# Sliding-window attention and a gated convolution layer on one core: tanh kept in PSUM, diagonals built later, and new parameters for the written-out order

## The chip, the cores and the metric

The kernel runs on one core of one Trainium2 chip. A core has a matrix engine (TensorE, PE in the profile), a vector engine (VectorE, DVE), a scalar engine (ScalarE, ACT), a general engine (GpSimd, POOL), and an engine that here only issues transfers (SyncE, SP). The metric is the device time of one launch in microseconds; the time given is the median of several runs. TensorE writes its results into PSUM, here one tensor `pf` of 4096 float32 columns that the kernel treats as eight banks of 512; everything else lies in SBUF.

## What is computed

Eight batches of windowed attention (eight heads, 576 positions, head size 64, each position sees the 32 on each side), and behind it a two-layer network whose hidden layer is gated by a three-tap convolution over positions:

```python
scores = np.where(np.abs(pos[:, None] - pos[None, :]) <= 32, q @ k.T / 8, -1e9)
x = softmax(scores) @ v                  # (8, 576, 512), heads side by side
h = np.maximum(x @ w_in, 0.0)            # 512 -> 1024
conv = sum(conv_w[t] * shifted(h, t - 1) for t in range(3))   # along the positions, zero at the ends
out = (h / (1.0 + np.exp(-conv))) @ w_out                     # 1024 -> 512
```

Inputs and output are float32; the matrix products are done in bfloat16. The sigmoid is taken as tanh: with `h` halved when it is evicted, `h * sigmoid(conv)` is `(tanh(conv / 2) + 1) * h / 2`.

## The kernel before, in words

**Units.** The 8 x 576 rows are cut into twelve chunks of 384 (`CH`), three to a pair of batches. The hidden layer is made transposed, d_ff on partitions, in eight blocks of 128 (`m`). One block of one chunk is a unit (`unit`, line 740); chunk 1 is worked in two halves of 192, because its first half needs batch 0 alone and its second batch 1. A unit is this chain:

- `ph`: 4 TensorE matmuls from `xT` and `w_in_sb` into a PSUM bank (`ps`), line 761
- `relu`: ScalarE evicts that bank into `hT`, halved, line 772
- `pc`: the convolution as matmuls with diagonal matrices (`diag_w`) into a second bank (`pc`), line 793. In chunks 0 and 1 all three taps; in the others (`TAP`, line 297) taps 0 and 2 only
- `tap`: for the others VectorE adds the middle tap into the bank, one scalar_tensor_tensor that reads and writes PSUM, line 804
- `tanh`: ScalarE reads the bank and writes `tn`, one of five float32 buffers in SBUF, line 813; the bank is free when it ends
- `gate`: VectorE makes `gT = (tn + 1) * hT`, line 818

When a chunk's eight units are there, `project` (line 829) multiplies `gT` by `w_out_sb` in three blocks of 128 rows, 8 matmuls of 512 columns each, ScalarE or VectorE evicts `y`, and SP stores it.

**Attention.** For each batch (`attention`, line 888) and each half of the heads: q and k are loaded into a ring of four buffers `st`, cast to bfloat16 (`cast_qk`, into `qkb`), transposed by TensorE (`transposes`, two banks for each of q and k) and evicted into `qkT`. `scores` takes three banks in a row for each of two parts, ScalarE writes exp into `attn`, VectorE multiplies by the mask. v is loaded into one buffer `vst`, cast into `ve` (`cast_v`), and copied once more, shifted by 64 partitions, into `vo` (`shift_v`, on VectorE). `values` multiplies, VectorE takes the reciprocal of the sums (`rec`) and scales into `xn`. `turn` makes `xT`: for batches 0 to 2 with TensorE and an eviction, for the others with a transposing DMA.

**What sets the order.** Nothing is scheduled while the kernel runs: each engine executes one fixed list. The lists come from `Planner` (lines 93 to 277), which runs when the kernel is built. Each piece of work is an `op` with a priority number (smaller is more urgent), a cost on each engine that may do it, the data that it reads and writes, the buffers that it takes and those that it uses. The planner plays the work through with modelled times: whenever an engine is free it takes the most urgent op that is ready and whose buffers, PSUM banks among them, are free at that moment. So the priority numbers, the costs and the buffer counts decide which instruction stands behind which. A bank is taken when the op that writes it is placed, and given back when the last op that uses it is done. Further rules of it:

- An op marked `two` isn't placed on VectorE while the plan has a `two` op on GpSimd, nor the other way round (`lock`). Casts, the masks, the shifted copies, the diagonals and, when `tn` is in SBUF, the gate are marked (line 825).
- On TensorE an op whose mode (`row`, `col`, none) differs from the last op's has `SWITCH` added to its priority.
- Where TensorE has nothing to do in the first 23 us (`FILL`), it is given dummy matmuls on zeros.
- A unit of chunk `c` has priority `8 c + m`, its later ops up to 0.7 more; the projection of chunk `c` has `8 (c + 1)` plus `PYAT`. A batch's attention lies between the two numbers of `place` (line 883), its steps at fixed tenths of that stretch; its loads come 12 before it.
- All loads and stores, and the transposing DMAs, are issued by SP in the planned order. SP waits for each one's buffer before it goes to the next.

The diagonals are made by `diag` ops (line 874), three multiplications of the identity each, for `m` from 0 to 7, right after the convolution weights have come, with priorities -20 to 5.

Of the kernel before, what the change touches and what calls it, by code (L numbers as in the profile page):

```python
# [92 lines left out]
class Planner:  # L93
# [4 lines left out]
    SWITCH = 0.1  # L98
# [30 lines left out]

    def run(self, start, filler, filler_until, late):  # L130
# [43 lines left out]
        for o in self.ops:  # L174
            if not o.left:
                push(0.0, "ready", o)
# [4 lines left out]
        while left or heap:  # L181
# [7 lines left out]
            for kind, x in batch:  # L189
                if kind == "ready":  # L190
                    offer(x)
                elif kind == "free":
                    x.give(now, 7, 1)
                elif kind == "done":
                    for s in x.uses:
                        s.users -= 1
                        if not s.users:
                            s.pool.give(now, s.index, s.span)
                    for n in x.after:
                        n.left -= 1  # L200
                        if not n.left:
                            push(now, "ready", n)
# [3 lines left out]
            for e in engines:  # L206
                while free[e] <= now + 1e-9:
                    best, blocked = None, False
                    other = {"DVE": "POOL", "POOL": "DVE"}.get(e, "PE")
                    for o in todo[e]:  # L210
                        if o in gone:
                            continue
                        if o.two and lock[other] > now + 1e-9:
                            blocked = True
                            continue
                        need = {}
                        for s in o.acquire:
# [3 lines left out]
                        key = o.prio + (self.SWITCH if e == "PE" and o.mode != mode else 0.0)  # L221
# [23 lines left out]
                    for n in o.follow:  # L245
                        n.left -= 1
                        if not n.left:
                            push(now, "ready", n)
# [32 lines left out]
START = {"SP": 0.9, "PE": 2.5, "ACT": 1.2, "DVE": 4.5, "POOL": 4.5}  # L281
FILL = 23.0
THIN = 2.0
NHT = 6
NTN, NQKT, NY = 5, 3, 3
NRING, NATTN, NGT, NQKB = 4, 3, 2, 6
LOADV1, LOADWO, CASTWO = -89.0, -89.5, 6.0
TN_SBUF = True
MASKER = ("DVE",)
ENGW = ("POOL", "ACT")  # L290
ENG1 = ("POOL", "DVE")
TAP0 = 1
AHEAD = 0
XD0 = 3
PYAT = (2.0, 4.5, 7.0)


def TAP(c, m):
    return c > TAP0


def XDMA(b):
    return b >= XD0


SH2, SHX = -2.0, -6.0
# [3 lines left out]
def kernel(  # L310
# [48 lines left out]
    ring = pool("st", NRING, [128, 2, 2, RP, 64], FP32)  # L359
    vst = sb.tile([128, NBLK, H, 64], FP32, name="vst")  # L360
    qkb = pool("qkb", NQKB, [128, RP, 2, 64], BF16)
    qkT = pool("qkT", NQKT, [128, 4, W], BF16)
    ve_b = [sb.tile([128, NBLK, H, 65], BF16, name=f"ve{i}") for i in range(2)]
    vo_b = [sb.tile([128, NBLK - 1, H, 65], BF16, name=f"vo{i}") for i in range(2)]
    attn_p = pool("attn", NATTN, [128, 36 * 64], BF16)
    rec_p = pool("rec", 4, [128, 4], FP32)
    xn_p = pool("xn", 2, [128, NBLK, H, 64], BF16)
    xT_b = [sb.tile([128, KC, 2, S], BF16, name=f"xT{i}") for i in range(2)]
    hT_p = [pool(f"hT{i}", NHT, [128, CH + (4 if i == 1 else 2)], BF16) for i in range(3)]
    gT_p = pool("gT", NGT, [128, MB, CH], BF16)  # L370
    tn_p = pool("tn", NTN, [128, CH], FP32) if TN_SBUF else None
    y_p = pool("y", NY, [128, d_model], FP32)
# [61 lines left out]
    pl.psum = pf  # L434
    op = pl.op

    def masker(b):
        costs = {"DVE": c_dve(1152, 2.0), "POOL": c_pool(1152, 2.6)}
        return {e: costs[e] for e in (("DVE",) if b < 2 else MASKER)}
# [65 lines left out]
    def cast_v(b, c, prio, engines):  # L505
        def emit(e):
            copier(e, ve_b[b % 2][:, c, :, 0:64], vst[:, c, :, :])
        op(f"cast v{b}{c}", cast_cost(512, engines), emit, prio,
           reads=[("vst", c)], writes=[("ve", b % 2, c)], two=True)

    def shift_v(b, c0, c1, prio):
# [3 lines left out]
        def emit_hi(e):  # L515
            vector.tensor_copy(out=vo[0:64, c0:c1], in_=ve[64:128, c0:c1])

        def emit_lo(e):
            vector.tensor_copy(out=vo[64:128, c0:c1], in_=ve[0:64, c0 + 1:c1 + 1])
        for emit, w, r in ((emit_hi, "hi", 0), (emit_lo, "lo", 1)):  # L520
            op(f"vo {w}{b}{c0}", {"DVE": c_dve(n, 4.0)}, emit, prio, two=True,
               reads=[("ve", b % 2, c + r) for c in range(c0, c1)],
# [42 lines left out]
    def transposes(b, i, y, prio, ahead):  # L565
# [4 lines left out]
        parts = 2 if ("qkb", b, i, y, 1) in pl.writer else 1  # L570
        turned = lambda x: ps[x].ap.bitcast(BF16)[:, 0:S]
        for n, js in enumerate(((0, 1, 2, 3), (4, 5, 6, 7, 8))):
            def emit(e, js=js):
                for j in js:
# [6 lines left out]
            o = op(f"tr {'qk'[y]}{b}{i}.{n}", {"PE": 0.03 * len(js)}, emit, prio, mode="row",  # L581
                   reads=[("qkb", b, i, y, min(n, parts - 1)), "ident"], writes=[("ptr", b, i, y, n)],
# [9 lines left out]
        for x in range(2):  # L592
            op(f"ev {'qk'[y]}{b}{i}.{x}", evac_cost(S), lambda e, x=x: emit_ev(e, x),
               prio + 0.05, reads=[("ptr", b, i, y, n) for n in range(2)], writes=[("qkT", b, i, y, x)],
# [49 lines left out]
    def values(b, i, c, prio, ahead, engines):  # L644
# [10 lines left out]
        def emit(e_):  # L655
# [12 lines left out]
            reads=[("attn", b, x, z) for x in halves for z in range(2)] + [("ve", b % 2, c)]  # L668
# [25 lines left out]
    def turn(b, c, prio, ahead):  # L694
# [5 lines left out]
        if XDMA(b):  # L700
# [39 lines left out]
    def unit(c, m, part, prio):  # L740
# [40 lines left out]
        op(f"relu {u}", {"ACT": c_act(n)}, emit_relu, prio + 0.1, reads=[("ph", u)], writes=[("h", u)], use=[ps, hT])  # L781
# [8 lines left out]
        on_dve = TAP(c, m)  # L790
# [20 lines left out]
        tn = Slot(tn_p) if TN_SBUF else pc  # L811

        def emit_tanh(e_):
            scalar.activation(tn.ap[:, 0:nc_], pc.ap[:, 0:nc_], AF.Tanh, bias=0.0, scale=1.0)
        op(f"tanh {u}", {"ACT": c_act(nc_)}, emit_tanh, prio + 0.6, reads=[("tap" if on_dve else "pc", u)],
           writes=[("tanh", u)], use=[pc], acquire=[tn] if TN_SBUF else [])

        def emit_gate(e_):
# [6 lines left out]
           use=[tn, hT, gT], two=TN_SBUF)  # L825
# [37 lines left out]
    def conv_weights(prio):  # L863
# [9 lines left out]
        for m in range(MB):  # L873
            def emit_d(e_, m=m):
# [6 lines left out]
               reads=["conv_w"], writes=[("diag", m)], two=True)  # L881

    place = {0: (-30.0, -10.0), 1: (1.0, 9.0), 2: (11.0 + SH2, 21.0 + SH2), 3: (21.0 + SHX, 31.0 + SHX),
             4: (34.0 + SHX, 46.0 + SHX), 5: (46.0 + SHX, 54.5 + SHX), 6: (57.0 + SHX, 69.0 + SHX),
             7: (69.0 + SHX, 78.5 + SHX)}
    loads = {b: -100.0 + 10.0 * b if b < 2 else place[b][0] - 12.0 for b in place}

    def attention(b):
        w0, w1 = place[b]
        early = b < 2  # L890
        ahead = 0 if b == 0 else AHEAD
        any3 = ("POOL", "DVE", "ACT")
        step = (w1 - w0) / 10.0
        lp = loads[b]
# [3 lines left out]
        for c in range(NBLK):  # L898
            load_v(b, c, (loads[b] if b != 1 else LOADV1) + 0.05 + 0.01 * c)
        for i in range(2):  # L900
            for y in range(2):
                cast_qk(b, i, y, w0 + step * (3 * i - 3.0), any3 if b == 0 else ENG1 if b == 1 else ("POOL",),
                        ((0, 4), (4, 9)) if b == 0 else ((0, 9),))
        for c in range(NBLK):
            cast_v(b, c, w0 + step * (2.0 + 0.2 * c), any3 if b == 0 else ENG1 if b == 1 else ("POOL",))
        if early:
            for c in range(NBLK - 1):
                shift_v(b, c, c + 1, w0 + step * (2.5 + 0.2 * c))
        else:
            shift_v(b, 0, NBLK - 1, w0 + step * 3.5)  # L910
        for i in range(2):
            for y in range(2):
                transposes(b, i, y, w0 + step * (2.8 * i + 0.9 * y), ahead)
            scores(b, i, w0 + step * (2.8 * i + 2.3), ahead)
        if early:
            for c in range(NBLK):
                for i in (range(2) if c < NBLK - 1 else (None,)):
                    values(b, i, c, w0 + step * (6.8 + 0.6 * c), ahead, ("DVE", "ACT"))
                turn(b, c, w0 + step * (7.4 + 0.6 * c), ahead)
        else:  # L920
            for i in range(2):
                for c in range(NBLK - 1):
                    values(b, i, c, w0 + step * (5.0 + 2.3 * i), ahead, ("DVE",))
            values(b, None, NBLK - 1, w0 + step * 7.3, ahead, ("DVE",))
            for c in range(NBLK):
                turn(b, c, w0 + step * 9.5, ahead)

    conv_weights(-60.0)
    for pr_ in range(B // 2):
        attention(2 * pr_)  # L930
        if pr_ == 0:
            for i in range(2):
                load_w("in", i, -99.0 + i * 0.1)
            for m in range(MB):
                cast_w("in", m, -9.0 + m, ("POOL", "DVE", "ACT"))
        attention(2 * pr_ + 1)
        if pr_ == 0:
            for i in range(2):
                load_w("out", i, LOADWO + i * 0.1)
            for m in range(MB):  # L940
                cast_w("out", m, CASTWO + 0.1 * m, ENGW)
        for c in range(3 * pr_, 3 * pr_ + 3):
# [3 lines left out]
            for i in range(3):  # L946
                project(c, i, 8.0 * (c + 1) + PYAT[i] if c < NCH - 1 else 8.0 * c + 3.6 + 0.1 * i)

    order = pl.run(START, (0.107, "filler", THIN), FILL, pf)
# [37 lines left out]
```

## Time and profile before

| | |
|---|---|
| runs | 246.98, 247.8, 248.75 us; median 247.8 |
| the profiled execution | 248.0 us; span from first to last instruction 246.2 us; granted TensorE clock 0.991 |
| busy | PE 224.6 us, weight loads 130.7, DVE 205.8, ACT 179.6, POOL 76.8 |
| moved | 32.52 MB read, 9.44 MB written, 65984 packets on the queue of SP |
| first unit's first matmul | at 25.8 us |
| last eviction of y | starts at 241.8 us |

In the profile L349 is the line of a helper through which every engine's operation passes, so groups are told apart by what they write and read: `gT<-tn,hT` is a gate. `[1.57 <-DVE qkT L349]` behind a row is idle time of the engine before it and what ended it. A row with `x12` is that many instructions, merged; its time runs from the first start to the last end. In tables of stages the columns are start and end, length, then busy microseconds of each engine with its number of instructions, the granted TensorE clock as a share, the mean busy share of the DMA engines (modelled, so it can pass 1), and GB/s.

### The profile page before, as it was taken

Reading aid. Unit: us, or ns where it says so; the run is one execution under the profiler, and the core shown is the slowest. Engines: PE = TensorE matmul, PEld = TensorE weight load, DVE = VectorE, ACT = ScalarE, POOL = GpSimd, SP = SyncE. Lnnn points to the kernel's source line nnn. Section 1 sums busy time; section 2 is a strip of 40 time slices with the busy share of each in tenths; the row PEclk is TensorE's granted clock in tenths of the full one; section 3 lists DMA queues with packets and bytes.
Section 4 is the critical chain, followed back from the end, with each engine's and each line's share of the span. In section 5 each row is a group of like instructions: output and inputs, shape, how many; then the busy total and the mean of one; then the engine's idle time right before and its main releaser. Section 6 shows DMA issues by size and latency. Waiting matters only on the chain.

```text
span 246.2 us, 7187 instructions
## 1 busy us (share of the span) xinstructions
PE 224.6 (91%) x2765; PEld 130.7 (53%) x2789; DVE 205.8 (84%) x457; ACT 179.6 (73%) x432; POOL 76.8 (31%) x108
## 2 busy tenths in 40 slices
PE   7787999699999599989999999999999999999981
PEld 4465557476655355455555555555555555555430
DVE  6989379999899979979998999899988985849342
ACT  3496999598997436889849858986698676757431
POOL 4326646866747313513650231350000000000000
PEclk9999999999999889999999999999999999999999
DMA  6999999999999169749973893961522233020213
GB/s 212 287 284 391 236 295 246 337 230 353 254 330 270 36 192 337 144 119 312 296 159 67 187 324 76 233 188 44 110 82 83 62 77 129 14 88 30 85 45 128
DMA packets 66054, 45.37 MB, mean 184 GB/s; under 512 B 51148, under 2 KB 51172, under 8 KB 66020
## 3 DMA queue, kind: packets, MB, share of 16 engines
q1 hardware_dynamic: 65984, 44.90, 65.5%
q8 instruction: 22, 0.36, 0.6%
q14 instruction: 12, 0.10, 0.1%
q10 hardware_dynamic: 36, 0.01, 0.1%
HBM read 32.52 MB, written 9.44 MB: 170 GB/s over the span
## 4 chain that ended last, share of the span: by engine, by line
PE 50%; DVE 6%; ACT 5%; issue 3%; ACTq 0%; DVEq 0%
PE pf L349 50%; ACT tn L349 2%; DVE pf L349 2%; ACT attn L349 2%; DVE xn L349 2%; DVE gT L349 1%; DVE rec L349 1%; ACT hT L349 1%; ACT qkT L349 1%; DVE attn L349 1%; ACTq L982 0%; ACT y L349 0%; DVEq L349 0%; ACTq L349 0%; DVE vo L349 0%
## 5 line engine op out<-in xcount | busy, mean ns | idle before, releaser
L349 PE MATMUL pf<-xT,w_in_sb 128*128 128x385 bf16 (+2 forms) x416 | 76.2, 317 | 0.8 <-DVE xn L349 0.6
L349 DVE SCALAR_TENSOR_TENSOR gT<-tn,hT 128x384 bf16<-128x384 f32 (+1 forms) x104 | 63.0, 627 | 12.2 <-ACT tn L349 11.4
L349 PE MATMUL pf<-w_out_sb,gT 128*128 128x512 bf16 x264 | 65.8, 381 | 2.6 <-DVE gT L349 0.9
L349 ACT ACTIVATE tn<-pf 128x384 f32<-128x384 f32 (+1 forms) x104 | 50.0, 515 | 18.8 <-DVE pf L349 17.9
L349 ACT ACTIVATE hT<-pf 128x385 bf16<-128x385 f32 (+2 forms) x104 | 50.6, 530 | 11.8 <-PE pf L349 10.9
L349 DVE SCALAR_TENSOR_TENSOR pf<-hT,conv_w_sb,pf 128x384 f32<-128x384 bf16 x80 | 47.7, 617 | 12.9 <-PE pf L349 11.9
L349 POOL TENSOR_SCALAR qkb<-st 128x1152 bf16<-128x1152 f32 (+2 forms) x32 | 38.7, 1211 | 50.6 <-DMA st<-in_k_dram 18.7
L349 PEld LDWEIGHTS <-w_in_sb 128*128 128x128 bf16 x416 | 38.6, 98 | 24.5 <-issue 2.5
L349 PE MATMUL pf<-hT,diag_w 128*128 128x384 bf16 (+1 forms) x232 | 48.1, 312 | 1.6 <-ACT hT L349 1.0
L349 PEld LDWEIGHTS <-gT 128*128 128x128 bf16 x288 | 27.6, 98 | 31.8 <-DVE gT L349 1.7
L349 ACT ACTIVATE attn<-pf 128x512 bf16<-128x512 f32 (+1 forms) x96 | 41.9, 555 | 2.9 <-PE pf L349 2.7
L349 POOL TENSOR_SCALAR ve<-vst 128x512 bf16<-128x512 f32 x38 | 28.1, 751 | 28.5 <-DMA vst<-in_v_dram 27.4
L349 ACT COPY y<-pf 128x512 f32<-128x512 f32 x32 | 18.9, 594 | 19.1 <-PE pf L349 18.6
L349 DVE TENSOR_TENSOR attn<-attn,mask 128x1152 bf16<-128x1152 bf16 x32 | 29.2, 916 | 2.1 <-ACT attn L349 1.6
L349 PEld LDWEIGHTS <-diag_w 128*128 128x128 bf16 x232 | 20.1, 98 | 15.1 <-issue 2.7
L349 ACT COPY qkT<-pf 128x576 bf16<-128x576 bf16 x41 | 27.2, 715 | 0.8 <-PE pf L349 0.7
L349 DVE TENSOR_TENSOR xn<-pf,rec 128x256 bf16<-128x256 f32 x64 | 23.3, 409 | 0.1
L349 PE MATMUL pf<-ve,attn 128*64 128x65 bf16 x320 | 15.7, 198 | 4.9 <-ACT attn L349 3.1
L349 PEld LDWEIGHTS <-attn 128*64 128x64 bf16 x576 | 12.3, 112 | 13.9 <-issue 6.0
L349 DVE COPY qkT<-pf 128x576 bf16<-128x576 bf16 x23 | 17.1, 751 | 2.9 <-PE pf L349 1.5
L349 DVE COPY vo<-ve 64x520 bf16<-64x520 bf16 (+1 forms) x28 | 17.7, 631 | 0.9
L349 PEld LDWEIGHTS <-qkT 64*128 64x128 bf16 x576 | 10.9, 95 | 10.5 <-issue 7.0
(39 smaller groups left out, 138.6 us busy)
## 6 DMA issues: line engine op xcount, KB each, us to landing
st<-in_q_dram SPq DMA_DIRECT2D x16, 576.0 KB, 6.2
st<-in_k_dram SPq DMA_DIRECT2D x16, 576.0 KB, 6.8
out_dram<-y SPq DMA_DIRECT2D x36, 256.0 KB, 2.7
vst<-in_v_dram SPq DMA_DIRECT2D x24, 256.0 KB, 8.5
vst<-in_v_dram SPq DMA_DIRECT2D x16, 192.0 KB, 5.8
st<-in_moe_w_in_dram SPq DMA_DIRECT2D x2, 1024.0 KB, 7.9
st<-in_moe_w_out_dram SPq DMA_DIRECT2D x2, 1024.0 KB, 9.1
xT<-xn SPq DMA_TRANSPOSE x30, 2.5
```

The lines of the kernel that those rows point to most:

```text
L349: return lambda *args, **kwargs: fixed(do(*args, **kwargs))
```

## The change

Buffers and plan, before and after:

| | before | after |
|---|---|---|
| `tn` buffers | 5 in SBUF | none: tanh is written back into the unit's own PSUM bank, and the gate reads it there; the gate is no longer marked `two` |
| `qkb`, `attn`, `xn`, `y` buffers | 6, 3, 2, 3 | 5, 4, 3, 4 |
| `hT`, `st`, `qkT`, `gT`, `rec` buffers | 6, 4, 3, 2, 4 | the same |
| diagonals for `m` of 2 to 7 | as soon as the weights are there | not before 22.25 in the plan's time |
| middle tap on VectorE | chunks 2 to 11, all eight blocks | the same, but for one block of chunk 8 |
| `SWITCH` | 0.1 | 0.05 |
| VectorE's start in the plan | 4.5 | 5.0 |
| planned cost of `relu` | for n columns | for n + 20 |
| batches 2 to 7 in the plan | 9-19, 15-25, 28-40, 40-48.5, 51-63, 63-72.5 | 10.0-20.0, 16.0-26.0, 30.3-41.2, 36.3-46.3, 51.7-63.7, 66.8-70.7 |
| batch 1 | 1-9 | -0.55-8.91 |
| loads ahead of a batch | 12 | 11.49 |
| casts of q and k, batch 1 / later | POOL or DVE / POOL | POOL / POOL or ACT |
| casts of v, batch 1 / later | POOL or DVE / POOL | POOL, DVE or ACT / POOL |
| casts of `w_in` / `w_out` | POOL, DVE or ACT / POOL or ACT | POOL or ACT / POOL, DVE or ACT |
| transposes of a half's q or k, after batch 0 | two ops (blocks 0-3, 4-8) | one op |
| `PYAT` | 2.0, 4.5, 7.0; last chunk 3.6 | 2.31, 4.75, 7.61; last chunk 2.16 |

The steps inside a batch (casts, transposes, scores, values, turning) also have new offsets for batch 0, batch 1 and the others. The core of the diff:

```diff
     def op(self, name, cost, emit, prio, reads=(), writes=(), reserve=(), acquire=(), use=(),
-           spare=0, mode=None, two=False, behind=None):
+           spare=0, mode=None, two=False, behind=None, early=0.0):
         o = Op(name, cost, emit, prio, list(acquire), spare, mode, two)
+        o.early = early
...
-                            push(now, "ready", n)
+                            push(max(now, n.early), "ready", n)
...
+P = {'start': {'SP': 0.9, 'PE': 2.5, 'ACT': 1.2, 'DVE': 5.0, 'POOL': 4.5},
...
+ 'diag': 22.25,
...
+ 'switch': 0.05,
+ 'hT': 6,
+ 'st': 4,
+ 'qkb': 5,
+ 'qkT': 3,
+ 'attn': 4,
+ 'gT': 2,
+ 'tn': 0,
+ 'y': 4,
+ 'xn': 3,
+ 'rec': 4,
...
+ 'at': ((-30.0, -10.0), (-0.55, 8.91), (10.03, 20.04), (15.96, 26.04), (30.29, 41.16), (36.31, 46.33), (51.71, 63.72),
+        (66.77, 70.71)),
...
+ 'lead': 11.49,
+ 'v1': -89.27,
+ 'w_in': (-99.0, -98.9),
+ 'w_out': -89.74,
+ 'cast_w_in': -0.86,
+ 'cast_w_out': -1.65,
+ 'e_qk': (('POOL', 'DVE', 'ACT'), ('POOL',), ('POOL', 'ACT')),
+ 'e_v': (('POOL', 'DVE', 'ACT'), ('POOL', 'DVE', 'ACT'), ('POOL',)),
+ 'e_vo': (('DVE',), ('DVE',), ('DVE',)),
+ 'e_mul': (('DVE', 'ACT'), ('DVE', 'ACT'), ('DVE',)),
...
+ 'tap': (0, 0, 8, 8, 8, 8, 8, 8, 7, 8, 8, 8),
+ 'xdma': 3,
+ 'py': (2.31, 4.75, 7.61),
+ 'py_last': 2.16}
...
-        tn = Slot(tn_p) if TN_SBUF else pc
+        tn = Slot(tn_p) if P["tn"] else pc
...
         op(f"tanh {u}", {"ACT": c_act(nc_)}, emit_tanh, prio + 0.6, reads=[("tap" if on_dve else "pc", u)],
-           writes=[("tanh", u)], use=[pc], acquire=[tn] if TN_SBUF else [])
+           writes=[("tanh", u)], use=[pc], acquire=[tn] if P["tn"] else [])
...
         op(f"gate {u}", {"DVE": c_dve(nc_)}, emit_gate, prio + 0.7, reads=[("tanh", u)], writes=[("g", c, m, part)],
-           use=[tn, hT, gT], two=TN_SBUF)
+           use=[tn, hT, gT], two=P["tn"])
...
             op(f"diag {m}", {"DVE": (0.31, 0.39)}, emit_d, -20.0 + m if m < 3 else m - 2.0,
-               reads=["conv_w"], writes=[("diag", m)], two=True)
+               reads=["conv_w"], writes=[("diag", m)], two=True, early=0.0 if m < 2 else P["diag"])
```

More of the change, by code (lines that the diff above doesn't have):

```diff
@@ L505, in cast_v, with emit @@
     def cast_v(b, c, prio, engines):
[L506 to L509, printed above, removed]
+        n = H // P["vparts"]
+        for z in range(P["vparts"]):
+            def emit(e, z=z):
+                copier(e, ve_b[b % 2][:, c, n * z:n * z + n, 0:64], vst[:, c, n * z:n * z + n, :])
+            op(f"cast v{b}{c}.{z}", cast_cost(512 // P["vparts"], engines), emit, prio,
+               reads=[("vst", c)], writes=[("ve", b % 2, c, z)], two=True)
     def shift_v(b, c0, c1, prio):
@@ L593, in transposes @@
             op(f"ev {'qk'[y]}{b}{i}.{x}", evac_cost(S), lambda e, x=x: emit_ev(e, x),
-               prio + 0.05, reads=[("ptr", b, i, y, n) for n in range(2)], writes=[("qkT", b, i, y, x)],
+               prio + 0.05, reads=[("ptr", b, i, y, n) for n in range(len(parts))], writes=[("qkT", b, i, y, x)],
                use=[ps[x], to])
@@ L890, in attention @@
         early = b < 2
-        ahead = 0 if b == 0 else AHEAD
-        any3 = ("POOL", "DVE", "ACT")
+        kind = min(b, 2)
+        ahead = P["ahead"][kind]
         step = (w1 - w0) / 10.0
-        lp = loads[b]
+        o = P["off"][kind]
+        at = lambda k, n=0.0: w0 + step * (o[k] + n)
+        lp = -100.0 + 10.0 * b if early else w0 - P["lead"]
         for i in range(2):
```

154 lines of the change are left out of this document (82 added, 72 removed).

## The prediction

> **What bounds the kernel now.** I read the page first, then the busy time by stage.
>
> ```profile
> span 246.2 us, 7187 instructions
> PE   7787999699999599989999999999999999999981
> ```
> ```profile
> 0.00:26.00 26.00, 20.45 (x307) 13.61 (x308) 21.76 (x78) 16.52 (x43) 11.81 (x41) 1.00 1.00 299
> 26.00:50.00 24.00, 21.68 (x328) 13.97 (x329) 18.97 (x34) 21.17 (x58) 16.07 (x18) 1.00 1.00 270
> 50.00:80.00 30.00, 28.68 (x499) 19.00 (x499) 28.57 (x58) 27.79 (x81) 19.55 (x21) 1.00 1.08 289
> 80.00:90.00 10.00, 7.19 (x75) 3.89 (x75) 8.29 (x18) 3.82 (x10) 2.41 (x5) 0.83 0.38 108
> 90.00:150.00 60.00, 57.55 (x738) 32.27 (x745) 56.61 (x124) 46.01 (x102) 21.47 (x21) 1.00 0.78 209
> 150.00:200.00 50.00, 49.14 (x619) 27.60 (x625) 46.20 (x104) 39.75 (x91) 5.52 (x7) 1.00 0.42 109
> 200.00:236.00 36.00, 35.85 (x191) 18.77 (x194) 21.39 (x39) 21.77 (x48) 0.00 (x0) 1.00 0.19 65
> ```
>
> Columns: stage, length, then busy us of PE, weight load, DVE, ACT, POOL, then granted clock, DMA share, GB/s. PE looks full from 50 us on, but its matmuls overlap, so I count its work by the distance between starts in the dense last stage:
>
> ```profile
> 204.88 1.89 PE L349 MATMUL pf<-w_out_sb,gT 128*128 128x512 bf16 x8
> 206.61 0.81 PE L349 MATMUL pf<-hT,diag_w 128*128 128x384 bf16 x4
> 207.26 2.14 PE L349 MATMUL pf<-xT,w_in_sb 128*128 128x385 bf16 x12
> ```
> ```profile
> 32.73 0.44 PE L349 MATMUL pf<-ident,qkb 64*128 64x64 bf16 x18
> ```
>
> Less the last one's own length (0.38, 0.33, 0.33, 0.19), a matmul costs 0.216, 0.16, 0.165 and 0.015 us. A unit (one of eight 128-row blocks of d_ff in a chunk) is 4 first-layer matmuls, 2 taps and 3 of the output projection: 0.66 + 0.32 + 0.65 = 1.63 us. There are 96 units (the 16 half units count as 8): 156 us. Chunks 0 and 1 have a third tap: 16 x 0.16 = 2.6. Attention per batch is 72 transposes, 72 scores and 72 value products; at 0.015 each 3.2 us, seven batches after the first 23. Together 182 us, in the 215 us between 26 and 241. So PE has about 33 us of hidden slack, and DVE, whose durations are real, is busy 94% from 50 to 80 and from 90 to 150, and 92% from 150 to 200, but 59% from 200 to 236. DVE's order of work is the bound from 50 to 200; PE alone is from 200 on; until 50 the loads are (DMA share 1.00).
>
> **Part 1: the gate reads tanh from PSUM.** Forms, then smallest/median/largest ns:
>
> ```profile
> L349 DVE SCALAR_TENSOR_TENSOR gT<-tn,hT 128x384 bf16<-128x384 f32 x88 | 53.9, 630 | 11.8 <-ACT tn L349 11.0
> L349 DVE SCALAR_TENSOR_TENSOR gT<-tn,hT 128x192 bf16<-128x192 f32 x16 | 9.2, 610 | 0.4 <-ACT tn L349 0.4
> ```
> ```profile
> L349 ACT ACTIVATE tn<-pf x104: 365/490/808, 28.5 to 239.7; 128x384 f32<-128x384 f32 x88, 128x192 f32<-128x192 f32 x16
> L349 DVE SCALAR_TENSOR_TENSOR gT<-tn,hT x104: 344/558/1498, 29.0 to 240.2; 128x384 bf16<-128x384 f32 x88, 128x192 bf16<-128x192 f32 x16
> L349 DVE SCALAR_TENSOR_TENSOR pf<-hT,conv_w_sb,pf x80: 600/617/625, 68.5 to 239.0; 128x384 f32<-128x384 bf16 x80
> L349 DVE TENSOR_TENSOR xn<-pf,rec x64: 387/414/424, 17.9 to 195.4; 128x256 bf16<-128x256 f32 x64
> L349 DVE COPY qkT<-pf x23: 743/751/761, 7.9 to 184.1; 128x576 bf16<-128x576 bf16 x23
> ```
>
> The gate has two SBUF inputs and spreads from 344 to 1498 ns; the tap, the scaling into xn and the DVE copy, each with one operand in PSUM, stay within 40 ns of each other, in the same stages, beside the same POOL casts. The long gates end where POOL ends:
>
> ```profile
> 24.00:50.00 26.00, 7.81 (x10) 5.75 (x13) 1.00 1.01 280
> 50.00:100.00 50.00, 14.28 (x23) 9.33 (x22) 0.97 0.91 248
> 100.00:150.00 50.00, 14.59 (x23) 11.51 (x24) 1.00 0.74 198
> 150.00:200.00 50.00, 13.59 (x25) 12.18 (x24) 1.00 0.42 109
> 200.00:240.00 40.00, 12.18 (x22) 11.09 (x23) 1.00 0.19 65
> ```
>
> These are the gates (DVE) and tanh (ACT) alone. After 200, where POOL does nothing, a gate takes 12.18/22 = 0.554 us. Up to 150 there are 56 gates in 36.68 us; 16 of them are halves. Undisturbed they would be 40 x 0.554 + 16 x 0.344 = 27.7 us, so 9.0 us are lost to POOL: 2.7 of them before 50 (8 x 0.554 + 2 x 0.344 = 5.1 of 7.81) and 6.3 from 50 to 150.
>
> With tanh in PSUM the gate has one SBUF input. Its price is not in the trace. Lower end 0.554: the DVE copy out of PSUM takes 751 - 600 = 151 ns over its 576 elements at 0.96 per ns, the quiet gate 154 over its 384, so a PSUM input adds nothing. Upper end 0.617, the tap, which also writes PSUM. I take 0.56, as the copy is the nearer row for what is read. ACT's write into PSUM is not shown either; from no change to the tap's extra 0.06 either way, so 104 x 0.06 = 6 us of ACT at most, spread over an engine with a fifth idle: taken as nothing. The Trainium skill, "Perfetto Trace Analysis", section "Optimizing Scalar/DVE Operations", speaks against the edit: it gives DVE about 60 ns of access overhead on SBUF and 125 on PSUM. By it each gate would be 65 ns dearer; the copy row above disagrees.
>
> Of the 9.0 us I put 6 on the path: those from 50 to 150, less 46 x 0.006 for my price. The part before 50 lies under the loads of batch 1:
>
> ```profile
> 43.01 1.60 POOL L349 TENSOR_SCALAR ve<-vst 128x512 bf16<-128x512 f32 x2
> 44.73 1.69 DVE L349 TENSOR_TENSOR attn<-attn,mask 128x1152 bf16<-128x1152 bf16 x1
> ```
>
> Its values are cast at 43.0, and the loads have no gap before that. **Gain 6 (bounds 0 and 9).**
>
> The price is a PSUM bank: it is now given back when the gate ends, at least 0.56 + 0.04 us later. From 50 to 200 there are 71 units: 71 x 0.6 = 43 bank us, 5.3 us if all eight banks were always the limit, 0 if never. At 50 us thirteen tanh stand against ten gates, so results are parked, each a bank from now on; but the gate no longer shares a lock with POOL in the plan (`two`), so it need not be put off. **Cost 1 (0 to 5.3).**
>
> **Part 2: diagonals later.** Eighteen of 24 go from 5-12 us to after 22.25 in the plan.
>
> ```profile
> 8.55 1.99 DVE L349 TENSOR_SCALAR diag_w<-ident,conv_w_sb 128x128 bf16<-128x128 bf16 x9
> 10.46 0.74 DVE L349 COPY qkT<-pf 128x576 bf16<-128x576 bf16 x1
> 11.26 0.41 PE L349 MATMUL pf<-qkT 64*128 64x64 bf16 x16 [1.57 <-DVE qkT L349]
> 28.98 2.93 DVE L349 SCALAR_TENSOR_TENSOR gT<-tn,hT 128x384 bf16<-128x384 f32 x3 [3.81 <-ACT tn L349]
> ```
>
> The last key copy queues behind nine of them, so the scores come up to 1.8 us earlier. The 18 then cost about 18 x 0.22 = 4 us in the 3.81 us in which DVE waits for the first tanh, the cover; without it a tap matmul would wait for them. What is late next is batch 1's values at 43, so an earlier first chunk mostly waits longer there. **Gain 0.5 (0 to 1.8).**
>
> **Part 3: places and loads.** The worst stall:
>
> ```profile
> 77.50 1.14 SPq L349 DMA_DIRECT2D vst<-in_v_dram  x2
> 78.47 2.24 DVE L349 TENSOR_TENSOR attn<-attn,mask 128x1152 bf16<-128x1152 bf16 x2
> 80.63 0.96 DVE L349 SCALAR_TENSOR_TENSOR gT<-tn,hT 128x384 bf16<-128x384 f32 x1
> 83.00 1.12 DVE L349 COPY vo<-ve 64x2080 bf16<-64x2080 bf16 x1
> 84.36 0.19 PE L349 MATMUL pf<-ve,attn 128*64 128x65 bf16 x1 [2.59 <-ACT attn L349]
> 85.40 0.37 SPq L349 DMA_DIRECT2D out_dram<-y  x1
> ```
>
> Batch 3's last value loads leave SP at 77.5, their shifted copy ends at 84.1, and PE idles 2.59 us; afterwards the clock is 0.83 over the stage, 1.7 us more. SP then sits until 85.4 on an output store, and batch 4's loads queue behind it. The change gives y, attn and xn one buffer more (4, 4, 3), moves batch 5 forward and batch 7 back, and lets ACT share the later q/k casts. **Gain 2.5 (0 to 4.3)**, more than half, since both the gate and the store that make this stall are touched. The rest of the plan (qkb 5 for 6, projection places, cheaper mode switches, transposes issued whole) reorders the same instructions; DVE must hand over its 92% somewhere, so from 5 lost to 6 won: **gain 1.** One tap of chunk 8 goes to PE, 0.16 us dearer there and 0.617 cheaper on DVE: nothing.
>
> Sum: 6 + 0.5 + 2.5 + 1 - 1 = 9. The profiled execution took 248.0 (1.8 around its span), 0.2 over the median 247.8. 248.0 - 9 = **239 us**.
>
> **Rivals.** (a) PSUM banks take over: three parked tanh hold three of eight banks while a score tile needs three in a row, so PE waits for gates. It decides as soon as gates lie a unit's time behind. Each of 71 units then holds 1.2 us longer, 10.7 us over eight banks, DVE's relief goes unfelt, parts 2 and 3 bring 3: 255.7 in full, 251.9 where half the stage is so. For it: the thirteen against ten. Against: the plan counts banks. Time **252**. (b) A PSUM read costs the gate 65 ns: from 50 to 150 its 46 gates take 32 x 0.617 + 14 x 0.41 = 25.5 of 28.87, a gain of 3.4, and the 25 to 200 lose 1.5: gain 2 in place of 6, **243**. Its chance is small because of the copy row. The Trainium skill's overheads, above, would give the same. (c) PE really is as full as its digits, so the relief of DVE is worth nothing and only part 2 and the rest of part 3 show: **246.5**. Against it: the 33 us. (d) The places spread DVE's work into the last stage, where it stands at 59%, and half of the 33 us goes: 248 - 16 = **232**. For it: batch 7 is moved back by about 4 units.
>
> **How the numbers follow.** Forecast 0.52, (a) 0.14, (b) 0.14, (c) 0.10, (d) 0.10. The forecast's own range is 234 to 244 (each gain at half or nearly whole). For 8 in 10 the range reaches over (d), (b) and (c): 230 to 250, leaving out (a) and a few lucky plans. A measurement here tells about 1% from no change. Faster by more: forecast, (b) and (d), less one in a hundred for their edges, 0.75; within: most of (c) and a little of (a), 0.11; slower: (a), 0.14.
>
> **What would show it.** Gates with a smallest-to-largest spread like the tap's and a median of 550 to 620; DVE busy 7 to 10 us less; scores of batch 0 from about 9.5; diagonals at 23 to 29; no PE idle of 2.5 us near 82. Wrong if the gates still spread, if DVE's busy share from 50 to 200 falls and PE gains nothing, or if PE's waits name the gate.

## The result and the profile after

The changed kernel takes 235.63 us (median of four runs, 233.99 to 235.96), the kernel before 248.28 in the runs beside it (246.98 to 249.68): ratio 0.9476, 95% interval 0.9406 to 0.9547, 5.2% or 13.0 us faster. Forecast were 239 us and a gain of 9. The experiments ran on several chips, each beside the kernel before; I compare their ratios to it, turned into microseconds with 248, and give the half width of the interval behind ± (for a difference of two ratios, the root of the sum of both squares). Ratios leave disturbed runs out, so one may differ a little from the quotient of two medians.

The page of the changed kernel, then its stages with the columns used above (PE, weight load, DVE, ACT, POOL, clock, DMA share, GB/s):

```profile
span 234.2 us, 7175 instructions
PE   7777999899999899999999999999999999999992
```
```profile
0.00:26.00 26.00, 19.94 (x314) 13.53 (x315) 19.89 (x66) 18.09 (x45) 12.14 (x42) 1.00 0.99 302
26.00:50.00 24.00, 22.40 (x339) 14.13 (x338) 21.75 (x58) 22.16 (x65) 13.58 (x16) 1.00 1.09 279
50.00:80.00 30.00, 28.97 (x472) 19.21 (x470) 27.10 (x59) 27.64 (x70) 14.34 (x17) 1.00 1.06 288
80.00:90.00 10.00, 9.51 (x145) 5.54 (x144) 9.78 (x23) 8.36 (x21) 3.57 (x5) 1.00 0.86 266
90.00:150.00 60.00, 59.44 (x768) 33.18 (x767) 56.46 (x129) 48.04 (x108) 15.96 (x18) 1.00 0.81 196
150.00:200.00 50.00, 49.91 (x607) 27.71 (x605) 43.28 (x99) 39.24 (x91) 3.21 (x5) 1.00 0.42 107
200.00:224.00 24.00, 24.00 (x132) 12.78 (x131) 15.18 (x27) 14.77 (x34) 0.00 (x0) 1.00 0.15 56
```

From 80 to 90 PE is busy 9.51 us where it was 7.19, and the clock is 1.00 where it was 0.83. DVE is still busy 94% from 90 to 150 (56.46 of 60), but gets more done. The forms of the gate, and smallest, median and largest duration of tanh, gate and tap:

```profile
L380 DVE SCALAR_TENSOR_TENSOR gT<-pf,hT 128x384 bf16<-128x384 f32 x88 | 46.5, 551 | 4.6 <-ACT pf L380 4.1
L380 DVE SCALAR_TENSOR_TENSOR gT<-pf,hT 128x192 bf16<-128x192 f32 x16 | 5.0, 346 | 1.3 <-ACT pf L380 1.2
```
```profile
L380 ACT ACTIVATE pf<-pf x104: 297/475/637, 27.3 to 226.9; 128x384 f32<-128x384 f32 x88, 128x192 f32<-128x192 f32 x16
L380 DVE SCALAR_TENSOR_TENSOR gT<-pf,hT x104: 319/548/558, 29.3 to 227.4; 128x384 bf16<-128x384 f32 x88, 128x192 bf16<-128x192 f32 x16
L380 DVE SCALAR_TENSOR_TENSOR pf<-hT,conv_w_sb,pf x79: 605/615/624, 67.0 to 226.2; 128x384 f32<-128x384 bf16 x79
```

The largest gate is 558 ns where it was 1498. The means fall from 630 to 551 (full units) and from 610 to 346 (halves).

How far the units come is seen by counting the first-layer matmuls (`w_in_sb`; columns PE, weight load, ACT, POOL, clock, DMA share, GB/s), the kernel before first, the changed one second:

```profile
24.00:50.00 26.00, 9.54 (x64) 5.59 (x64) 1.20 (x2) 0.00 (x0) 1.00 1.01 280
50.00:90.00 40.00, 10.15 (x62) 5.45 (x63) 0.00 (x0) 0.00 (x0) 0.96 0.91 244
90.00:150.00 60.00, 22.11 (x116) 10.82 (x114) 0.00 (x0) 0.00 (x0) 1.00 0.78 209
150.00:200.00 50.00, 19.93 (x100) 9.29 (x100) 0.00 (x0) 0.00 (x0) 1.00 0.42 109
```
```profile
24.00:50.00 26.00, 9.59 (x64) 5.61 (x64) 1.15 (x2) 0.00 (x0) 1.00 1.09 288
50.00:90.00 40.00, 13.10 (x81) 7.24 (x82) 0.00 (x0) 0.00 (x0) 1.00 1.01 282
90.00:150.00 60.00, 21.86 (x114) 10.78 (x113) 0.00 (x0) 0.00 (x0) 1.00 0.81 196
150.00:200.00 50.00, 19.62 (x108) 10.09 (x105) 0.00 (x0) 0.00 (x0) 1.00 0.42 107
```

By 200 us 342 had run before and 367 after. Four belong to a unit of about 1.63 us of PE, so the 25 are worth about 10 us. The rest of the 12 us between the two spans is at the end. In this pair nineteen of the 25 come from 50 to 90 and eight from 150 to 200, but that split is not safe: a second profile of the kernel before (`before_py_last_new`, whose edit leaves every list as it was) has the same 342 by 200 us, divided otherwise:

```profile
50.00:90.00 40.00, 12.05 (x76) 6.63 (x76) 0.00 (x0) 0.00 (x0) 1.00 0.89 251
90.00:150.00 60.00, 20.37 (x106) 9.88 (x104) 0.00 (x0) 0.00 (x0) 1.00 0.77 204
150.00:200.00 50.00, 19.10 (x96) 8.89 (x96) 0.00 (x0) 0.00 (x0) 1.00 0.42 109
```

### The profile page after: what moved, and what is told of

It is laid out like the page before. It is cut to its first block, busy times and chain, and to the rows that moved or that the text cites. A ratio compares the mean times of both kernels' runs of the same rounds, so it can differ in the third digit from the quotient of the medians.

```text
span 234.2 us, 7175 instructions
## 1 busy us (share of the span) xinstructions
PE 219.8 (94%) x2790; PEld 128.5 (55%) x2790; DVE 197.5 (84%) x463; ACT 181.6 (78%) x432; POOL 62.8 (27%) x101
## 4 chain that ended last, share of the span: by engine, by line
PE 65%; DVE 19%; ACT 5%; DMA 3%; issue 3%; SPq 1%; ACTq 0%; POOL 0%; DVEq 0%; POOLq 0%
PE pf L380 65%; DVE gT L380 5%; DVE attn L380 4%; DMA vst<-in_v_dram 3%; DVE pf L380 3%; DVE diag_w L380 3%; ACT attn L380 2%; DVE vo L380 2%; DVE xn L380 1%; SPq L380 1%; ACT pf L380 1%; ACT xn L380 1%; DVE rec L380 1%; DVE qkT L380 1%; DVE xT L380 1%
## 5 line engine op out<-in xcount | busy, mean ns | idle before, releaser
L380 PE MATMUL pf<-xT,w_in_sb 128*128 128x385 bf16 (+2 forms) x416 | 73.9, 315 | 1.4 <-DVE gT L380 0.9
L380 ACT ACTIVATE pf<-pf 128x384 f32<-128x384 f32 (+1 forms) x104 | 47.0, 478 | 13.1 <-DVE pf L380 12.3
L380 ACT ACTIVATE hT<-pf 128x385 bf16<-128x385 f32 (+2 forms) x104 | 48.1, 501 | 11.3 <-PE pf L380 10.1
L380 DVE SCALAR_TENSOR_TENSOR gT<-pf,hT 128x384 bf16<-128x384 f32 (+1 forms) x104 | 51.4, 519 | 5.9 <-ACT pf L380 5.3
L380 PE MATMUL pf<-hT,diag_w 128*128 128x384 bf16 (+1 forms) x233 | 46.3, 310 | 0.7 <-DVE gT L380 0.3
L380 POOL TENSOR_SCALAR qkb<-st 128x1152 bf16<-128x1152 f32 (+1 forms) x27 | 29.6, 1097 | 57.2 <-DMA st<-in_q_dram 30.5
L380 POOL TENSOR_SCALAR ve<-vst 128x512 bf16<-128x512 f32 x37 | 25.0, 682 | 30.4 <-DMA vst<-in_v_dram 24.6
L380 ACT COPY qkT<-pf 128x576 bf16<-128x576 bf16 x36 | 22.7, 660 | 1.8 <-PE pf L380 1.7
L380 DVE COPY qkT<-pf 128x576 bf16<-128x576 bf16 x28 | 20.4, 748 | 2.9 <-PE pf L380 2.3
L380 DVE COPY vo<-ve 64x520 bf16<-64x520 bf16 (+1 forms) x28 | 15.4, 549 | 2.0 <-POOL ve L380 1.2
L380 PE MATMUL pf<-qkT 64*128 64x64 bf16 x576 | 14.3, 191 | 1.6 <-DVE qkT L380 0.9
```

Of the source, the lines that this page charges most:

```text
L380: return lambda *args, **kwargs: fixed(do(*args, **kwargs))
```

## The experiments

**Tanh in SBUF again, every list unchanged.** Each unit takes a free one of four float32 tiles; no instruction changes its place.

```diff
+    tn_free = [sb.tile([128, CH], FP32, name=f"tn{i}") for i in range(4)]
+    tn_of = {}
...
-            scalar.activation(tn.ap[:, 0:nc_], pc.ap[:, 0:nc_], AF.Tanh, bias=0.0, scale=1.0)
+            tn_of[u] = tn_free.pop(0)
+            scalar.activation(tn_of[u][:, 0:nc_], pc.ap[:, 0:nc_], AF.Tanh, bias=0.0, scale=1.0)
...
-                out=gT.ap[:, m, g0:g0 + nc_].rearrange("p (i x) -> p i x", x=HW), in0=in3(tn.ap), scalar=1.0,
+                out=gT.ap[:, m, g0:g0 + nc_].rearrange("p (i x) -> p i x", x=HW), in0=in3(tn_of[u]), scalar=1.0,
                 in1=taps(1), op0=ALU.add, op1=ALU.mult,
             )
+            tn_free.append(tn_of[u])
```

Expected: 

> The changed kernel with every engine's list kept as it is; only tanh goes to one of four float32 buffers in SBUF and the gate reads it there. Theory 1 (the gate's freedom from POOL is what counts): gates spread again to 1 us and more, DVE busy about 10 us more, time up by 6 us to about 241.5. Theory 2 (the new order counts, not the gate's own length): gates spread as well, but the time rises by less than 1.5 us, to at most 237.

Measured: 241.5 us (239.01 to 242.24), ratio 0.9744 (0.9681 to 0.9806). Against 0.9476 that is 6.6 us slower, ± 2.3. The gates:

```profile
L380 DVE SCALAR_TENSOR_TENSOR gT<-tn,hT 128x384 bf16<-128x384 f32 x88 | 49.2, 581 | 4.7 <-ACT tn L380 3.9
L380 DVE SCALAR_TENSOR_TENSOR gT<-tn,hT 128x192 bf16<-128x192 f32 x16 | 7.7, 518 | 1.3 <-ACT tn L380 1.2
```
```profile
L380 ACT ACTIVATE tn<-pf x104: 325/490/685, 27.6 to 230.1; 128x384 f32<-128x384 f32 x88, 128x192 f32<-128x192 f32 x16
L380 DVE SCALAR_TENSOR_TENSOR gT<-tn,hT x104: 322/551/1403, 29.6 to 230.6; 128x384 bf16<-128x384 f32 x88, 128x192 bf16<-128x192 f32 x16
```

The quiet gate is the same (median 551 against 548), the largest is 1403 (1498 in the kernel before), and the means give 88 x 0.030 + 16 x 0.172 = 5.4 us more of DVE; its busy time goes from 197.5 to 202.8. Nothing else differs between the two programs but the tile of zeros for the dummy matmuls, which is half as wide to make room; they read the same 256 columns of it. One of the long gates, and the cast beside it:

```profile
114.29 1.15 POOL L380 TENSOR_SCALAR qkb<-st 128x1152 bf16<-128x1152 f32 x1 [3.43 <-PE pf L380]
114.44 1.40 DVE L380 SCALAR_TENSOR_TENSOR gT<-tn,hT 128x384 bf16<-128x384 f32 x1
```

The gate starts inside the cast and ends 0.40 us behind it. Nine of the 104 gates in this trace take more than 0.65 us (19 in the kernel before). Each of them has a POOL instruction beside it and ends 0.20 us (halves) or 0.40 us (full units) behind the end of one, and no gate without one beside it takes more than 0.56 us. In the changed kernel 33 gates have one beside them, and none takes more than 0.558. So the slow gates come from the SBUF operand beside POOL's casts.

The 6.6 us of the ratios agree with the 5.4 us of DVE only within their interval: the profiled execution, the fastest of the four, is 3.0 us longer in span than that of the changed kernel (237.2 against 234.2). Theory 1 holds, with its size open between about 3 and 9 us; theory 2 (at most 237) does not, as the fastest run took 239.01.

**The same, planned anew** (`tn` 4, the gate marked `two`).

```diff
- 'tn': 0,
+ 'tn': 4,
...
-    zero = sb.tile([128, 512], BF16, name="zero")
+    zero = sb.tile([128, 256], BF16, name="zero")
```

Expected: 

> The changed kernel planned anew with four tanh buffers in SBUF, the gate marked as sharing the port again, all else as changed (the zero tile halved for room). Theory 1: as in the same order, about 242, or a little less because the plan can put gates aside while POOL casts. Theory 2: about 237. If the parameters were fitted to tanh in PSUM, their luck is lost as well: 244 or more.

Measured: 244.0 us (240.07 to 245.56), ratio 0.9769 (0.9676 to 0.9862), 7.3 slower than the changed kernel, ± 2.9. Here a bank comes free when tanh ends, as in the kernel before, so this is what the whole edit brings, bank included. It agrees with the same order; whether fitted parameters lose anything beyond that stays within the interval.

**Tanh in PSUM in the kernel before.**

```diff
-TN_SBUF = True
+TN_SBUF = False
```

Expected: 

> The kernel before with tanh written back to PSUM and the gate reading it there, planned anew, nothing else. Theory 1: about 242, six less than before. Theory 2: 247 to 249, no change. Banks as the limit: 250 or more, with TensorE waiting for gates.

Measured: 244.56 us (242.79 to 246.22), ratio 0.9878 (0.9803 to 0.9953): 3.0 us faster, ± 1.9. That is half of theory 1's six, and neither no change nor slower. DVE's busy time falls by 7.9 us (205.8 to 197.9), so much of it does not reach the end. Its stage from 80 to 90, and who TensorE waits for:

```profile
80.00:90.00 10.00, 9.31 (x159) 5.62 (x159) 9.20 (x22) 8.27 (x21) 1.74 (x3) 1.00 0.58 158
```
```profile
PE pf L349 <- DVE gT L349: 2.8, 6, 0.8
```

With the old places, PE is busy 9.31 of these 10 us. So the disappearance of this stall is no proof that the new places removed it.

**Diagonals early in the changed kernel.**

```diff
- 'diag': 22.25,
+ 'diag': 0.0,
```

Expected: 

> The changed kernel with the diagonals planned as soon as the weights are there. By the prediction's part 2 the late diagonals give 0.5 us: 236.1. If the first scores set the start of the first unit: 1.8 more, 237.4. If the late diagonals stand in the way of batch 1 instead, because they meet POOL's casts: 235 or less.

Measured: 237.55 us (236.63 to 238.62), ratio 0.9603 (0.9557 to 0.9650), 3.1 us slower, ± 2.1: more than forecast. But planned anew every engine's list is another one, which the next two avoid.

**Only the diagonals moved, in either kernel.** In the changed kernel back to where they were; in the kernel before behind the last eviction of `xT` of batch 0.

```diff
+    first = next(t for t, _, e, o in order if o != "filler" and o.name == "diag 1")
+    evs = sorted(t for t, _, e, o in order if o != "filler" and e == "DVE" and o.name[:3] == "ev ")
+    at = {2: first, 3: first, 4: evs[0], 5: evs[0], 6: evs[0], 7: evs[1]}
+    order = [(at[int(o.name[5:])] + 1e-6, n, e, o) if o != "filler" and o.name[:5] == "diag " and int(o.name[5:]) > 1
+             else (t, n, e, o) for t, n, e, o in order]
     order.sort(key=lambda x: (x[0], x[1]))
```
```diff
+    order = [(max(t, 22.25), n, e, o) if o != "filler" and o.name[:5] == "diag " and int(o.name[5:]) > 1 else (t, n, e, o)
+             for t, n, e, o in order]
     order.sort(key=lambda x: (x[0], x[1]))
```

Expected, changed kernel: 

> The changed kernel's lists kept, only the eighteen late diagonals moved to where they stood before (12, 9 and 3 among the first copies of qkT). Prediction: the first scores and the first unit come later by up to 1.8 us, of which 0.5 is seen at the end: 236.1. If it is the late diagonals themselves that cost (they meet POOL's casts at 22 to 29): 235 or less. If the 2 us that the kernel with early diagonals planned anew was slower come from the diagonals and not from the rest of that plan: 237.5.

Expected, kernel before: 

> The kernel before, lists kept, only the eighteen diagonals moved behind the last eviction of xT of batch 0. Prediction: 0.5 us faster, 247.8. If the start of the first unit carries through: 1.8 faster, 246.5. If nothing before the loads of batch 1 counts: 248.3.

Measured: in the changed kernel 236.53 us (233.34 to 238.87), ratio 0.9522 (0.9405 to 0.9638): 1.1 slower, ± 3.4, which tells nothing apart. In the kernel before 245.27 (243.16 to 247.65, ten runs), ratio 0.9931 (0.9886 to 0.9977): 1.7 us faster, ± 1.1. Its first scores, diagonals and first unit:

```profile
8.19 0.76 DVE L349 COPY qkT<-pf 128x576 bf16<-128x576 bf16 x1 [1.01 <-PE pf L349]
8.85 0.83 PE L349 MATMUL pf<-qkT 64*128 64x64 bf16 x36
23.22 5.87 DVE L349 TENSOR_SCALAR diag_w<-ident,conv_w_sb 128x128 bf16<-128x128 bf16 x18
23.78 2.12 PE L349 MATMUL pf<-xT,w_in_sb 128*128 128x385 bf16 x12
```

The key copy starts at 8.19, where it started at 10.46, and the scores run from 8.85 in one piece. The eighteen diagonals end at 29.09 and take 5.87 us, not 4: the median is 0.242 us, but the longest, beside a cast on POOL, takes 1.16. The first unit starts at 23.78; the kernel before starts it at 25.82 in one profile and 25.27 in another (next experiment). That is 1.5 to 2 us earlier, and by the ratios the end comes 1.7 ± 1.1 earlier.

**The last chunk's projections.** In both kernels the other kernel's number.

```diff
-                project(c, i, 8.0 * (c + 1) + PYAT[i] if c < NCH - 1 else 8.0 * c + 3.6 + 0.1 * i)
+                project(c, i, 8.0 * (c + 1) + PYAT[i] if c < NCH - 1 else 8.0 * c + 2.16 + 0.1 * i)
```
```diff
- 'py_last': 2.16}
+ 'py_last': 3.6}
```

Expected, kernel before: 

> The kernel before with the last chunk's projections at 8 c + 2.16 in place of 8 c + 3.6, nothing else. The prediction had no term for the tail: 248.3. New theory from the two traces: before, TensorE idles about 2 us between the last units (the last first-layer matmul at 237.1 and the last projection at 241.6), since projections that were ready had been issued ahead of the last units or behind them; the earlier number takes 2 us off: 246.3.

Expected, changed kernel: 

> The changed kernel with the last chunk's projections at 8 c + 3.6 again. New theory: 2 us slower, 237.6. If the tail is no matter of this number: 235.6.

Measured: 247.05 us (246.12 to 248.79, ten runs), ratio 1.0009 (0.9970 to 1.0048), and 234.9 us (234.5 to 235.82), ratio 0.9537 (0.9470 to 0.9605). In the changed kernel only the ends of three lists differ, from 213 us of the plan on. By the ratios this is 1.5 us slower, ± 2.4, which leaves the 2 us possible; the profiles do not. The same tanh, one of the last ahead of that point, starts at 210.12 us here and at 210.25 in the changed kernel, and the spans are 234.0 and 234.2 us: the ends are equally long, and the theory about this number falls. The run is thus nearly a second measure of the changed kernel, and it warns that every difference to 0.9476 in this document may be up to about 1.5 us too large. In the kernel before the edit leaves all five lists as they were, so it doesn't test the theory; it is the same program once more, and a measure of what two profiles of one program differ by: its first unit starts at 25.27, not 25.82, and its stage from 80 to 90 looks like this:

```profile
80.00:90.00 10.00, 7.14 (x69) 4.14 (x68) 9.62 (x21) 5.43 (x13) 4.46 (x6) 1.00 0.65 181
```

PE is as idle as in the first profile (7.19), but the clock stays at 1.00. The two spans are 244.5 and 246.2 us, and in between the same instruction can lie further off: the eviction of `y` at 100.40 in the first profile is at 97.06 here. Smaller differences between two single traces say nothing.

**The other projections' places.** The tail itself is real. Its last TensorE rows, before and after:

```profile
236.61 0.82 PE L349 MATMUL pf<-xT,w_in_sb 128*128 128x385 bf16 x4
238.14 0.49 PE L349 MATMUL pf<-hT,diag_w 128*128 128x384 bf16 x2 [0.70 <-ACT hT L349]
238.46 1.47 PE L349 MATMUL pf<-w_out_sb,gT 128*128 128x512 bf16 x6
240.82 0.82 PE L349 MATMUL pf<-w_out_sb,gT 128*128 128x512 bf16 x3 [0.89 <-DVE gT L349]
```
```profile
224.21 1.46 PE L380 MATMUL pf<-w_out_sb,gT 128*128 128x512 bf16 x6
225.51 0.49 PE L380 MATMUL pf<-hT,diag_w 128*128 128x384 bf16 x2
225.83 3.83 PE L380 MATMUL pf<-w_out_sb,gT 128*128 128x512 bf16 x17
```

Before, the last unit runs dry: PE waits 0.70 us for its eviction and 0.89 for its gate. After, 17 projection matmuls stand behind the last tap matmuls and cover tap, tanh and gate. In the kernel before the last chunk but one has its third projection at 88 + 7.0 = 95.0, the number of the last unit; at 95.61 it is less urgent.

```diff
-PYAT = (2.0, 4.5, 7.0)
+PYAT = (2.31, 4.75, 7.61)
```

Expected: 

> The kernel before with the projection places 2.31, 4.75, 7.61 in place of 2.0, 4.5, 7.0, nothing else. Theory: the third projection of the last chunk but one (7.0) ties with the last unit and is issued ahead of it; at 7.61 it stands behind it and covers its eviction, tap, tanh and gate, so the 0.70 and 0.89 us in which TensorE idles at the end go, and the time falls by 1.6 to 2.0: about 246.4. Rival: the earlier chunks' projections move too and the rest of the order changes for the worse, 248 or more.

Measured: 243.93 us (242.15 to 246.34, ten runs), ratio 0.9858 (0.9819 to 0.9898): 3.5 us faster, ± 1.0. Its end:

```profile
233.43 0.81 PE L349 MATMUL pf<-hT,diag_w 128*128 128x384 bf16 x4
234.08 3.83 PE L349 MATMUL pf<-w_out_sb,gT 128*128 128x512 bf16 x17
```

The two waits are gone, as the theory has it, worth 1.6 us by their rows. The other 1.9, if the 3.5 is no less, must come from the other chunks, whose lists the edit changes too. By 200 us its profile has run 342 first-layer matmuls, as many as the kernel before, so the units are not further; where it comes from, I have not separated.

**Three parts in the kernel before.** Tanh in PSUM, diagonals from 22.25 in the plan, the new projection places; nothing else.

```diff
-TN_SBUF = True
+TN_SBUF = False
...
-PYAT = (2.0, 4.5, 7.0)
+PYAT = (2.31, 4.75, 7.61)
...
-               reads=["conv_w"], writes=[("diag", m)], two=True)
+               reads=["conv_w"], writes=[("diag", m)], two=True, early=0.0 if m < 2 else 22.25)
```

Expected: 

> The kernel before with tanh in PSUM, the diagonals not before 22.25 in the plan, and the new projection places; old places of the batches, old buffers and engines. If the parts add up (5.9 of the gate in one order, 1.7 of the diagonals, 2.0 of the tail): 238.7, and the new batch places and buffers are worth 3. If replanning loses half of the gate's part again, as tanh in PSUM alone did (3 in place of 6): 241.7, and places, buffers and engines are worth 6.

Measured: 239.38 us (239.31 to 239.46), ratio 0.9702 (0.9662 to 0.9741): 7.4 us faster, ± 1.0. The three alone gave 3.0 + 1.7 + 3.5 = 8.2, so within their intervals they add up, with tanh at the three that it brings in this plan and not at the six of the changed order. To the changed kernel 5.6 us remain, ± 2.0.

**Old places, old buffers in the changed kernel.**

```diff
- 'at': ((-30.0, -10.0), (-0.55, 8.91), (10.03, 20.04), (15.96, 26.04), (30.29, 41.16), (36.31, 46.33), (51.71, 63.72),
-        (66.77, 70.71)),
+ 'at': ((-30.0, -10.0), (1.0, 9.0), (9.0, 19.0), (15.0, 25.0), (28.0, 40.0), (40.0, 48.5), (51.0, 63.0),
+        (63.0, 72.5)),
```
```diff
- 'qkb': 5,
+ 'qkb': 6,
...
- 'attn': 4,
+ 'attn': 3,
...
- 'y': 4,
- 'xn': 3,
+ 'y': 3,
+ 'xn': 2,
```

Expected, places: 

> The changed kernel with the old stretches of the plan for the eight batches (1-9, 9-19, 15-25, 28-40, 40-48.5, 51-63, 63-72.5), the new offsets within them. Prediction, part 3: these places and the buffers together give 3.5; with the places alone gone 2 us slower, 237.6. If the places are the rest of the gain: 240 or more. If only buffers and offsets count: 235.6.

Expected, buffers: 

> The changed kernel with 6, 3, 2 and 3 buffers for qkb, attn, xn and y, as before. Prediction, part 3: 1.5 us slower, 237.1, with output stores and value loads that wait on SP again. If the buffers don't count: 235.6. If the places were fitted to these buffers: 240 or more.

Measured: with the old places 237.39 us (237.07 to 238.91), ratio 0.9633 (0.9581 to 0.9685), 3.9 us slower, ± 2.2; with the old buffers 238.15 (237.38 to 238.91), ratio 0.9654 (0.9596 to 0.9711), 4.4 slower, ± 2.3. First-layer matmuls late in the kernel, old places first, old buffers second:

```profile
90.00:150.00 60.00, 21.68 (x112) 10.63 (x112) 0.00 (x0) 0.00 (x0) 1.00 0.79 197
150.00:200.00 50.00, 18.93 (x99) 9.36 (x100) 0.00 (x0) 0.00 (x0) 1.00 0.41 107
```
```profile
90.00:150.00 60.00, 20.05 (x108) 10.31 (x108) 0.00 (x0) 0.00 (x0) 1.00 0.84 208
150.00:200.00 50.00, 17.74 (x96) 9.28 (x97) 0.00 (x0) 0.00 (x0) 1.00 0.33 83
```

With the old places the changed kernel is 2 matmuls behind from 90 to 150 and 9 from 150 to 200, where its 108 become 99, the count of the kernel before (100). With the old buffers it is 6 and 12 behind. In sum over the time to 200 us, the safer measure, they are 12 and 15 behind (355 and 352 against 367), where the second profile of nearly the same program (the last chunk's projections, above) has 368. With the old buffers SP also waits longer for evictions of `y` again, as expected: 59.7 us for those on ScalarE and 6.8 for one on VectorE, against 50.1 and none. So by the ratios both are worth about 4 us each as long as the other is new; the two together with the offsets, engines and the smaller numbers are worth 5.6 ± 2.0, less than the 8.3 of both, but not by more than the intervals. Which of the four buffers it is, and which batch's place, was not tried, nor the offsets and the engines by themselves.

## Why the prediction was right, and where its terms were off

**What bounds the kernel: borne out, but not everywhere.** The forecast was DVE's order of work from 50 to 200. Shortening only gates, in lists otherwise the same, moved the end by 6.6 ± 2.3 us for 5.4 of DVE, so rival (c), PE as full as its digits, is out. In the old plan 7.9 us less of DVE moved it by 3.0 ± 1.9 only: there DVE was not alone.

**The gate: right in length and cause.** Price taken 0.56 us; measured 0.551, and 0.346 for halves. A gate with one operand in PSUM is untouched by POOL (largest 558). The Trainium skill, "SBUF — State Buffer", section "Who interferes with whom", has it that a VectorE instruction with at most one SBUF input, outside the modes that use two ports, does not contend with GpSimd, while one with two SBUF inputs contends with a GpSimd instruction that reads SBUF; the 1403 against 558 ns of the two programs in one order agree. Rival (b), the dearer PSUM read, is out: the quiet medians are 551 with tanh in SBUF and 548 with it in PSUM. The overhead of 125 ns for PSUM against 60, which the prediction quoted from the Trainium skill, "Perfetto Trace Analysis", is not seen on this input.

**What it brings: 6 forecast, 6.6 ± 2.3 in the changed order, but not for the reason given.** The forecast counted what the gates lost in the old order. In the changed order they lose 5.4 us in all, as fewer of them meet a cast. In the test with the lists kept the bank is held to the end of the gate on both sides, so it has the gate's part alone. With its bank the edit was forecast at 6 - 1 = 5; planned anew, it brought 3.0 ± 1.9 under the old parameters and 7.3 ± 2.9 under the new. The step "Of the 9.0 us I put 6 on the path: those from 50 to 150" was too generous for the old plan, and that the 6 fits in the new one is in part luck.

**The bank: 1 forecast, 2.4 us of waits found, their price open.** TensorE now does wait for gates, which the prediction had named as a sign against it; the first of these waits behind the total:

```profile
PE pf L380 <- DVE gT L380: 2.4, 7, 0.6
29.89 0.81 PE L380 MATMUL pf<-xT,w_in_sb 128*128 128x385 bf16 x4 [0.54 <-DVE gT L380]
```

None of the seven matmuls reads `gT`, so what they wait for is a bank. The one such wait before (0.89 us at 240.82) is another thing, a projection that waits for its input. How much of the 2.4 us reaches the end was not measured. Rival (a), 252 us with banks as the limit, did not come; its sum gives parts 2 and 3 three us where the forecast's own terms are 0.5 + 2.5 + 1 = 4.

**ACT's write into PSUM: nothing forecast, a little less found.** In lists otherwise the same, tanh's median is 475 ns into PSUM and 490 into SBUF.

**The diagonals: mis-sized.** 0.5 forecast, 1.7 ± 1.1 measured in the kernel before. The step that failed is "an earlier first chunk mostly waits longer" at the values of batch 1: by the profiles the earlier start came through, 1.5 to 2 us at the first unit and 1.2 to 2.9 at the end (a span of 243.3 against 244.5 and 246.2). The copy and the scores did move as described (8.19 and 8.85). The cover was not quite enough: eighteen diagonals were put at 4 us and took 5.87 there; in the changed kernel fifteen take 5.24, and the first gate starts at 29.30 though the first tanh starts at 27.3 (before: 28.98 and 28.5):

```profile
24.13 5.24 DVE L380 TENSOR_SCALAR diag_w<-ident,conv_w_sb 128x128 bf16<-128x128 bf16 x15
29.30 1.01 DVE L380 SCALAR_TENSOR_TENSOR gT<-pf,hT 128x384 bf16<-128x384 f32 x2
```

**Places and loads: too small, and its evidence wrong.** Part 3 had 2.5 for the stall near 82 and 1 for the rest of the plan, projection places included. Measured: 3.5 ± 1.0 for the projection places and 5.6 ± 2.0 for places, buffers, engines and offsets. The stall near 82 is gone, but it also goes with tanh alone, and with the three parts under the old places and buffers PE is busy 9.88 of the 10 us. What the new places, buffers, engines and offsets bring shows in the count by 200 us: with the three parts alone 350 first-layer matmuls have run, 17 fewer than the 367. In which stage they are gained, single profiles don't settle. The tail, 1.6 us of waits that stood in the trace of before at 238 and 240 us, had no term at all.

**The sum: near, by terms that cancel.** Forecast were 5 (tanh with its bank), 0.5 (diagonals) and 3.5 (places, loads and the rest of the plan), 9 in all. Measured were 3.0, 1.7 and, for that rest, 3.5 (projection places) and 5.6 (places, buffers, engines, offsets), less the 0.8 by which three parts together bring less than alone: 13.0. As the 5.6 is a difference to the whole, the sum closes by construction and proves nothing. So 2 too much was given to tanh and 6 too little to the rest, net 4.0 (3.4 from 239 to the median of 235.63). That the time came out this near to 239 is in part luck. Rival (d) said that work would be spread into the last stage; it wasn't: DVE is busy 63% there (15.18 of 24) after 59%.

## What to carry to other kernels

When one engine's duration spreads by a factor while a like instruction beside it doesn't, compare their operands: an intermediate that is made from PSUM and used once may stay in PSUM, if a bank can be spared for half a microsecond more. Then look at the end of the trace for itself: independent work issued behind the last chain covers its waits. And a planned order makes parts interact, so test an edit with the lists kept wherever that can be done: planned anew, the same edit was worth 3.0 ± 1.9 us under one set of numbers and 7.3 ± 2.9 under another.

## What the runs showed that was not expected

ScalarE is no slower into PSUM than into SBUF, it is 15 ns faster (475 against 490 at the median); the Trainium skill, "ScalarE: Activation LUTs", section "Step-by-step: what each stage is for", says that PSUM is its lower-latency destination, and the rows agree. The diagonals, tensor_scalar from SBUF to SBUF with a pointer scalar, lose to POOL as the gate did:

```profile
L380 DVE TENSOR_SCALAR diag_w<-ident,conv_w_sb x24: 241/243/1194, 5.2 to 40.0; 128x128 bf16<-128x128 bf16 x24
```

Most take 243 ns and start 0.16 us apart; the three long ones among the fifteen above, 1.14 to 1.19 us, each lie beside one of POOL's casts. The 0.22 us that the prediction took for one was no undisturbed price: of its nine, one took 0.70 beside a cast.
